# A list schedule computed at build time, DMA transposes and an earlier start for a two-layer attention and feed-forward kernel

## The chip, the cores and the metric

The kernel runs on one core of a Trainium2 chip. The metric is the device time of one execution in microseconds. Runs of one program agree within 0.3%. Short names: TensorE is PE in the profile (PEld is its weight load), VectorE is DVE, ScalarE is ACT, and SP is the engine that issues the DMAs.

## The reference

Two identical layers over x of 2,048 tokens by 1,024 columns, bf16. Each layer is local attention (32 heads of 32; a query looks at 8 keys, 2 tokens apart, backwards) and a gated feed-forward (SwiGLU) of width 3,584. Both layers use the same weights.

```
def _A_ref(x, wqkv, wo):                      # W = 8, dil = 2
    q, k, v = (x @ wqkv) split into 32 heads
    logits = einsum("bhsd,bhswd->bhsw", q, k[s - 2*w]) / sqrt(32), masked before token 0
    return softmax(logits) weighted sum of v[s - 2*w], heads joined, @ wo
def _B_ref(x, w1, w3, w2):
    return (silu(x @ w1) * (x @ w3)) @ w2
...
for _ in range(2):
    x = x + _A_ref(_layernorm(x), wqkv, wo)
    x = x + _B_ref(_layernorm(x), w1, w3, w2)
```

The pieces run in chunks of 512 tokens: Q (layer norm, q, k and v), T (attention itself, in halves of 256 tokens, on VectorE, then the projection with wo on TensorE) and B (layer norm, feed-forward). The matmuls of all chunks are 7,424 of 128x128 weights on 512 columns.

## The kernel before

A tile framework allots buffers from pools and orders the instructions of each engine; the kernel gives priorities. The parts that the change touches:

```
psQ = ...tile_pool(name="psQ", bufs=2, space=PSUM)     # PSUM banks: q/k/v and transposes
psB = ...tile_pool(name="psB", bufs=4, space=PSUM)     # feed-forward
psT = ...tile_pool(name="psT", bufs=1, space=PSUM)     # attention projection, two banks
...
def ln_chunk(c, psum):
    ...                                                # statistics, rstd
    for j in range(TPC):
        nc.vector.tensor_scalar(xn[:], x_sb[:, n, :], mv[:, j, 0:1], rstd[:, j:j + 1], ...)
        for kk in range(KT):
            nc.tensor.transpose(pT[:, kk, :], xn[:, kk * P:(kk + 1) * P], ident[:])
        nc.scalar.copy(xnT[:, :, j * P:(j + 1) * P], pT[:])
def q_stage(l, c, ln_next=None):
    for which in range(3):                             # q, k, v; weights loaded anew for each chunk
        ...
                for kk in range(KT):
                    nc.tensor.matmul(ps[:], lhsT=w[:, kk, t::KT], rhs=xnT[:, kk, :], ...)
                nc.scalar.copy(sgt[:, t - t0, :], ps[:])
            nc.sync.dma_start(qkv_d[l][which][...], sgt[:])   # to DRAM, read back by t_stage
def t_stage(l, tcx):
    nc.sync.dma_start(qT[:], qkv_d[l][0][...]); ...    # k and v likewise
    ...                                                # about 80 VectorE operations, oT
            for t in range(KT):
                nc.tensor.matmul(ps[:, hh, :], lhsT=oT[...], rhs=wo[...], ...)
def b_stage(c, last):
    for (f0, f1) in [(0, 16), (16, NF)]:               # hidden width in two parts
        ...                                            # w1, w3, Silu, product into hT, w2, x += acc
```

## Time and profile before

| | before |
|---|---|
| time, median of 3 | 1,693.61 us (1,693.15 to 1,695.7) |
| profiled span, granted clock | 1,695.0 us, 0.995 |
| N=512 matmuls x pitch | 7,424 x 215.9 ns = 1,602.5 us |
| first q matmul; first attention multiply | 13.45 us; 59.39 us |

From the page, part 1 (busy time, share of the span, instructions):

```profile
PE 1661.5 (98%) x7952; PEld 823.1 (49%) x7952; DVE 1142.3 (67%) x1930; ACT 378.7 (22%) x561; POOL 1.9 (0%) x12
```

TensorE is the bound, but 98% does not say by how much it could shrink: busy times of single matmuls overlap. The Trainium skill, too, calls the matmul busy share a poor measure of distance to the roof ("Perfetto Trace Analysis", "Identifying the Most-Contended Engine"). The chain of waits gives a better rule. Its columns are start, duration, what:

```profile
46.24 13.99 PE ps L197 x64
60.86 10.93 DMA qkv_d_2_168<-sgt
616.95 27.63 PE acc L308 x128
```

128 matmuls in 27.63 us are 215.9 ns each, the pace at which nothing is lost. So 1,602.5 us of the span are matmuls that neither kernel can avoid, and 92 us are the rest. The chain also shows the early part passing through a DMA that stores v: attention's inputs go through DRAM.

What TensorE waited for (in all, times, longest):

```profile
PE pT L132 <- DVE xn L128: 9.6, 9, 2.7
PE po L268 <- DVE oT L172: 6.5, 13, 2.2
PE ps L197 <- ACT sgt L199: 3.2, 3, 2.0
PE pT L157 <- DVE xn L154: 2.5, 3, 0.9
PE pT L132 <- DVE x_sb L313: 1.4, 1, 1.4
```

Busy time by stretch (stretch, length, then engines with counts, granted clock, DMA share, GB/s):

```profile
14.00:160.00 146.00, 137.72 (x678) 87.62 (x677) 116.31 (x205) 54.17 (x86) 0.00 (x0) 0.97 0.82 276
160.00:420.00 260.00, 256.26 (x1225) 125.94 (x1224) 254.74 (x431) 62.40 (x89) 0.00 (x0) 1.00 0.54 169
700.00:930.00 230.00, 226.85 (x1112) 114.85 (x1110) 146.36 (x248) 54.90 (x80) 0.00 (x0) 1.00 0.53 168
```

Read the counts, not the busy times. Of the 678 in the first stretch 96 are transposes (about 57 ns each), so the work is 582 x 0.2159 + 96 x 0.057 = 131 us in 146: 15 us lost. Done for all stretches after the start, the loss is 48 us. Note also that VectorE is busy for 254.7 of 260 us in the second stretch.

### The profile page before, as it was taken

What the parts mean: (1) busy time and instruction counts of PE and PEld (TensorE: products, weight loads), DVE (VectorE), ACT (ScalarE), POOL (GpSimd) and SP (SyncE); (2) the same over time, 40 slices, a digit from 0 to 9 for tenths busy, and PEclk for the clock granted to TensorE, in tenths of its full rate; (3) what the DMA queues carried; (4) which work ended last, traced back from release to release, by engine and by line L of the source; (5) the groups of instructions that cost most, each with busy time, mean ns of one, the idle gap of its engine ahead of it and who ended that gap; (6) DMA issues with size and microseconds to landing.
All of it is one profiled execution on the core that took longest, in us unless ns stands there. A gap on an engine that the chain in (4) does not pass through costs nothing.

```text
span 1695.0 us, 19762 instructions
## 1 busy us (share of the span) xinstructions
PE 1661.5 (98%) x7952; PEld 823.1 (49%) x7952; DVE 1142.3 (67%) x1930; ACT 378.7 (22%) x561; POOL 1.9 (0%) x12
## 2 busy tenths in 40 slices
PE   8999999999999999999999999999999999999999
PEld 5655644444444444554445544455444554444444
DVE  5699999999996821229982399813997159952112
ACT  3433422212213101132022321223212221121100
POOL 0000000000000000000000000000000000000000
PEclk9999999999999999999999999999999999999999
DMA  9976655554454244475434754356542654435443
GB/s 315 325 242 201 223 167 160 174 164 149 142 170 148 95 160 146 149 241 182 128 122 155 244 179 148 97 195 229 185 145 95 200 161 151 149 108 191 149 149 99
DMA packets 282891, 289.51 MB, mean 171 GB/s; under 512 B 6192, under 2 KB 256048, under 8 KB 282672
## 3 DMA queue, kind: packets, MB, share of 16 engines
q1 hardware_dynamic: 282800, 288.25, 52.7%
q8 instruction: 62, 1.02, 0.2%
q14 instruction: 29, 0.24, 0.0%
HBM read 258.87 MB, written 29.36 MB: 170 GB/s over the span
## 4 chain that ended last, share of the span: by engine, by line
PE 51%; DVE 39%; DMA 4%; issue 4%; ACT 2%; DVEq 0%; SPq 0%; ACTq 0%
PE acc L308 15%; PE pu L290 11%; PE pg L286 11%; PE ps L197 10%; DVE tm L261 6%; DVE pr L220 5%; DVE hT L295 4%; PE po L268 3%; DVE pr L170 3%; DVE tm L170 3%; DVE st L119 2%; DVE pr L171 2%; DVE tm L171 2%; DMA qkv_d_1_170<-sgt 2%; DVE x_sb L313 1%
## 5 line engine op out<-in xcount | busy, mean ns | idle before, releaser
L290 PE MATMUL pu<-xnT,w3t 128*128 128x512 bf16 x1792 | 430.9, 380 | 0.0
L286 PE MATMUL pg<-xnT,w1t 128*128 128x512 bf16 x1792 | 430.8, 380 | 0.1
L308 PE MATMUL acc<-w2t,hT 128*128 128x512 bf16 x1792 | 392.7, 379 | 0.8 <-DVE hT L295 0.8
L197 PE MATMUL ps<-xnT,wqkv 128*128 128x512 bf16 x1536 | 340.8, 382 | 4.8 <-ACT sgt L199 3.2
L294 ACT ACTIVATE sg<-pg 128x512 bf16<-128x512 f32 x224 | 133.7, 597 | 679.5 <-PE pg L286 662.9
L197 PEld LDWEIGHTS <-wqkv 128*128 128x128 bf16 x1536 | 220.2, 144 | 118.3 <-issue 10.3
L286 PEld LDWEIGHTS <-w1t 128*128 128x128 bf16 x1792 | 175.5, 98 | 209.0 <-issue 2.2
L290 PEld LDWEIGHTS <-w3t 128*128 128x128 bf16 x1792 | 175.5, 98 | 208.4 <-issue 1.6
L308 PEld LDWEIGHTS <-hT 128*128 128x128 bf16 x1792 | 174.9, 98 | 209.5 <-DVE hT L295 1.5
L220 DVE TENSOR_TENSOR pr<-qT,kT 128x2048 bf16<-128x2048 bf16 x128 | 153.6, 1213 | 170.1 <-DMA kT<-qkv_d_1_170 158.2
L295 DVE TENSOR_TENSOR hT<-sg,pu 128x512 bf16<-128x512 bf16 x224 | 152.0, 679 | 170.8 <-PE pu L290 162.7
L313 DVE TENSOR_TENSOR x_sb<-x_sb,acc 128x512 bf16<-128x512 bf16 x128 | 87.0, 681 | 147.6 <-PE acc L308 147.6
L199 ACT CAST sgt<-ps 128x512 bf16<-128x512 f32 x192 | 112.0, 586 | 229.4 <-PE ps L197 200.9
L261 DVE TENSOR_TENSOR tm<-At,vT 128x2048 bf16<-128x2048 bf16 x128 | 152.8, 1215 | 0.1
L268 PE MATMUL po<-wo,oT 128*128 128x512 bf16 x512 | 127.6, 381 | 7.8 <-DVE oT L172 6.5
L133 ACT COPY xnT<-pT 128x1024 bf16<-128x1024 bf16 x60 | 57.7, 1024 | 158.1 <-PE pT L132 153.3
L268 PEld LDWEIGHTS <-oT 128*128 128x128 bf16 x512 | 48.9, 97 | 89.8 <-DVE oT L172 39.5
L170 DVE TENSOR_TENSOR pr<-pr 128x1024 bf16<-128x1024 bf16 x128 | 86.0, 678 | 0.0
L170 DVE TENSOR_TENSOR tm<-tm 128x1024 bf16<-128x1024 bf16 x128 | 84.6, 682 | 0.0
L119 DVE BATCH_NORM_STATS2 st<-x_sb 128x6 f32<-128x512 bf16 x120 | 75.7, 672 | 6.8 <-DMA x_sb<-in_A_x_dram 6.5
L272 DVE TENSOR_TENSOR x_sb<-x_sb,po 128x1024 bf16<-128x1024 bf16 x32 | 38.7, 1210 | 25.1 <-PE po L268 25.1
L171 DVE TENSOR_TENSOR pr<-pr 128x512 bf16<-128x512 bf16 x128 | 52.2, 414 | 0.1
(203 smaller groups left out, 514.5 us busy)
## 6 DMA issues: line engine op xcount, KB each, us to landing
w1t<-in_B_w_dram SPq DMA_DIRECT2D x56, 1024.0 KB, 5.3
w3t<-in_B_w_dram SPq DMA_DIRECT2D x56, 1024.0 KB, 7.2
w2t<-in_B_w_dram SPq DMA_DIRECT2D x48, 1024.0 KB, 5.4
wqkv<-in_A_wqkv_dram SPq DMA_DIRECT2D x23, 2048.0 KB, 8.1
w2t<-in_B_w_dram SPq DMA_DIRECT2D x16, 512.0 KB, 5.1
qkv_d_0_166<-sgt SPq DMA_DIRECT2D x16, 256.0 KB, 4.8
qkv_d_1_167<-sgt SPq DMA_DIRECT2D x16, 256.0 KB, 5.0
qT<-qkv_d_0_166 SPq DMA_DIRECT2D x8, 512.0 KB, 4.8
```

The source lines that it names most:

```text
L170: nc.vector.tensor_tensor(buf[:, 0:4, :], buf[:, 0:4, :], buf[:, 4:8, :], op=ALU.add)
L171: nc.vector.tensor_tensor(buf[:, 0:2, :], buf[:, 0:2, :], buf[:, 2:4, :], op=ALU.add)
L197: nc.tensor.matmul(ps[:], lhsT=w[:, kk, t::KT], rhs=xnT[:, kk, :], start=(kk == 0), stop=(kk == KT - 1))
L199: nc.scalar.copy(sgt[:, t - t0, :], ps[:])
L220: nc.vector.tensor_tensor(pr[:], qT[:], kT[:, :, k0:k0 + TCH], op=ALU.mult)
L261: nc.vector.tensor_tensor(tm[:], At[:], win, op=ALU.mult)
L268: nc.tensor.matmul(ps[:, hh, :], lhsT=oT[:, t, j * P:(j + 1) * P], rhs=wo[:, t, hh * 512:(hh + 1) * 512], start=(t == 0), stop=(t == KT - 1))
L286: nc.tensor.matmul(pg[:], lhsT=w1t[:, kk, fi * P:(fi + 1) * P], rhs=xnT[:, kk, :], start=(kk == 0), stop=(kk == KT - 1))
L290: nc.tensor.matmul(pu[:], lhsT=w3t[:, kk, fi * P:(fi + 1) * P], rhs=xnT[:, kk, :], start=(kk == 0), stop=(kk == KT - 1))
L294: nc.scalar.activation(sg[:], pg[:], ACTF.Silu)
L295: nc.vector.tensor_tensor(hT[:, g0 + fi - f0, :], sg[:], pu[:], op=ALU.mult)
L308: nc.tensor.matmul(acc[:], lhsT=hT[:, f - f0, j * P:(j + 1) * P], rhs=w2ts[(f - f0) // 8][:, (f - f0) % 8, :], start=(f == f0), stop=(f == ...
```

## The change

The intent: write every engine's order down at build time. A small list scheduler is told a duration for each operation, plays the engines, the DMA queue and eight PSUM banks forward, and emits the operations in order of their planned start; the framework adds the semaphores only. With it come other changes. One of them is not in the cut below: the order of the stages. From the first layer's third chunk to the second layer's second, each feed-forward stage comes one chunk of q/k/v and attention later than before. The diff, cut to its core:

```
+class Program:                       # add(): reads, writes -> dependencies; place(): the plan
+    def place(self, n_banks=8, rate=330e3):
+        ...                           # earliest start first; PE picks among the heads of its lanes
+            if op.table not in (None, table):
+                t = max(t + 1.28, ready_at[op])          # ScalarE table load in the clock
+        placed.sort(key=lambda o: (o.start, o.seq))
...
-                for kk in range(KT):
-                    nc.tensor.transpose(pT[:, kk, :], xn[:, kk * P:(kk + 1) * P], ident[:])
-                nc.scalar.copy(xnT[:, :, j * P:(j + 1) * P], pT[:])
+            dma(256, xb[:, :, j * P:(j + 1) * P], xn[j][:], [("xn", j)], [("xnT", b, j)], 0, transpose=True)
...
+    def q_first():
+        load_x(0, 0, 2)
+        wslots[0] = q_weights(0, "k")
+        load_x(0, 2, 4)
+        b = ln(0, first=True)                             # this chunk still transposes on TensorE
+        order = [(0, 0, 5), (1, 0, 5), (0, 5, 8), (1, 5, 8), (2, 0, 8), (3, 0, 8)]
+        ...                                               # q of one 128-token tile at a time: 256 N=128 matmuls
+        wslots[1] = q_weights(1, "s")
+        load_x(1)
+        load_x(2, 0, 2)                                   # x ahead of wv
+        wslots[2] = q_weights(2, "s")                     # layer 0's weights stay for all four chunks
...
+                if keep:                                  # first chunk's k and v also straight to kT, vT
+                    evac(act, 0.4, lambda _, a=a, m=m: nc.scalar.copy(keep[1][:, m, HALO:], bank[a.bank][:, 0:TCH]), ...)
...
+                op = mm8(a, [(oT[oh][...], wo[...]) ...], ..., lane=1)   # projection: a lane of its own
...
-    fsplits = [(0, 16), (16, NF)] if NF > 16 else [(0, NF)]
+    hT = alloc("hT", [P, NF, CH])                         # hidden width in one part
+                pieces = pieces[:-1] + [(TPC - 1, 0, 256), (TPC - 1, 256, 128), (TPC - 1, 384, 128)]   # last tile
+    with tc.manual_schedule():
+        for op in pr.place():
+            op.emit(op)
```

## The prediction

> **What bounds it now.** TensorE. The page gives PE 98% busy, DVE 67%, ACT 22%, DMA queue 53%. There are 7,424 N=512 matmuls (groups of instructions); in the chain of waits 128 take 27.63 us, 215.9 ns each: 1,602.5 us that cannot go away. The other 92 us of the 1,695 us span: about 13.5 us before the first projection matmul (timeline), 480 later PE transposes (16 in 0.94 us in the timeline, 58 ns each, so 28 us), 3.8 us after the last matmul, and about 48 us of small losses. Counting matmuls by window (count times 216 or 58 ns against window length), the losses after the start are 15 us in 14-160 us (clock 0.97 there), 2 to 7 us in each later window, mostly at layer norms and output projections (waits: transposes on xn 9.6 us, projections on oT 6.5, ps on evacuation 3.2). VectorE sets the pace only early (254.7 of 260 us busy in 160-420); its first attention multiply waits until 59.4 us for k's round trip through DRAM.
>
> **What the change does.**
> - Layer-norm transposes after the first chunk go to DMA: 480 PE transposes (28 us of TensorE) and 60 ScalarE copies (58 us, off the path) go; 60 transfers of 256 KB are added. No trace here shows one. The Trainium skill, "DMA: Bandwidth & Descriptors", "Latency and other measured facts", states 261 GB/s for them; estimated 1 us each plus the few us to landing of ordinary ones.
> - A static list schedule on each engine, eight PSUM banks shared by all uses. Attention's projections come in blocks of 32 when all inputs should be ready: most of the 48 us goes. Its vector durations match the trace (1.22 against 1.21 us); the trace's pitch is shorter still (1.14), so real VectorE should run ahead of its plan and TensorE seldom wait for it.
> - Start: the first q is done token tile by token tile, 256 N=128 matmuls (about 15 us against 13.8), but begins when the first of four xnT tiles is there (about 9.7 us, from the first copy in the timeline), not all four (13.45), so q should end about 24.5 us against 28.9: 4 us. First k and v go straight into the attention tiles (16 extra copies of about 0.4 us, hidden): first attention multiply at about 40 us instead of 59.4. Off TensorE's path, but VectorE is then ahead of the feed-forward.
> - One feed-forward split instead of two: 64 fewer residual adds (44 us VectorE, hidden). Layer 0's qkv weights are loaded once instead of four times (18 MB less).
> - Tail: last tile cut into 256, 128, 128 columns: about 1 us.
>
> **Sum.** 24.5 us to the end of first q, plus 7,360 x 0.2159 = 1,588.8, plus 3 us tail = 1,616; plus remaining stalls, estimated 10 us (first feed-forward stage: only about 15 us of matmuls lie between the last attention projection and it, to cover adds, norm, four DMA transposes). **1,627 us**, 4% faster. Range 1,617 to 1,645. Chances: faster by over 2% 0.93, within 2% 0.06, slower by over 2% 0.01.
>
> **What would show it.** PE transposes left: 32. First q matmul at 9 to 11 us; k's first matmul at about 25 us; first pr at 38 to 42 us. DVE about 1,100 us, ACT about 325 us, DMA about 270 MB. PE's waits below 20 us in total, the largest before the first feed-forward stage.
>
> **What would make it wrong.** DMA transposes much slower than estimated, or blocking the in-order DMA queue: waits on xnT at stage starts, late weights. TensorE blocks placed too early, waiting on oT. TensorE's clock dropping in the broken-up start.

## The result

The changed kernel takes 1,617.26 us (median of 4 runs, 1,617.0 to 1,617.75) against 1,694.65 us for the one before in the same rounds. The ratio is 0.9543 (95% interval 0.9529 to 0.9556): 4.6% faster, 77.4 us between the medians. All ratios are the mean time of one kernel's fast runs over that of the other's fast runs of the same rounds, so they are not quite the ratio of the medians quoted. The outputs are correct. The time lies in the predicted range, but only 0.3 us above its lower end: 9.7 us under the point forecast.

Page, part 1:

```profile
PE 1610.0 (100%) x7716; PEld 764.4 (47%) x7716; DVE 1120.2 (69%) x1900; ACT 328.9 (20%) x519; POOL 1.9 (0%) x12
```

The chain of waits, which had 1,843 pieces before, now has 23:

```profile
23 pieces in order of time: start us, us, what
...
5.71 6.18 DMA x<-in_A_x_dram
...
24.28 1588.69 PE bank L355 x7416
1612.97 0.02 issue
1612.99 0.29 DVE x L600
```

The line of 1,588.69 us is the result in one line: from the first k matmul to the last, TensorE was never found waiting. These 7,416 matmuls hold 7,332 of N=512 and 84 narrower ones of the cut last tile. As columns they equal 7,360 of N=512, and 7,360 x 215.9 ns = 1,588.8 us. All TensorE waits (in all, times, longest) are before 16 us:

```profile
PE bank L334 <- DVE xn L320: 1.3, 2, 1.1
PE bank L278 <- DVE warm L274: 1.2, 1, 1.2
PE bank L438 <- ACT xnT L339: 0.4, 1, 0.4
```

The same stretches as before:

```profile
14.00:160.00 146.00, 145.74 (x807) 89.91 (x805) 121.72 (x219) 57.22 (x108) 0.00 (x0) 1.00 0.61 181
160.00:420.00 260.00, 260.00 (x1207) 122.71 (x1206) 229.41 (x391) 53.99 (x79) 0.00 (x0) 1.00 0.60 179
700.00:930.00 230.00, 230.00 (x1068) 104.22 (x1066) 197.08 (x337) 47.40 (x72) 0.00 (x0) 1.00 0.57 176
```

In the third stretch 1,068 matmuls fit where 1,016 and 96 transposes did before, and the clock is 1.00 throughout. The start, from the timeline (start, duration, what, and in brackets the idle time before it):

```profile
6.78 1.32 PE L334 MATMUL bank<-ident,xn 128*128 128x128 bf16 x16 [1.07 <-DVE xn L320]
8.50 6.41 PE L438 MATMUL bank<-xnT,slot 128*128 128x128 bf16 x112 [0.40 <-ACT xnT L339]
15.17 0.62 PE L334 MATMUL bank<-ident,xn 128*128 128x128 bf16 x8 [0.26 <-DVE xn L320]
24.11 36.22 PE L355 MATMUL bank<-xnT,slot 128*128 128x512 bf16 x167
```

q begins at 8.50 us and k at 24.1 us. After the last matmul 2.7 us remain to the end (3.8 before).

### The profile page after: what moved, and what is told of

Its sections match the earlier page's. It is cut to its first block, busy times and chain, and to the rows that moved or that the text cites. A ratio compares the mean times of both kernels' runs of the same rounds, so it can differ in the third digit from the quotient of the medians.

```text
span 1615.7 us, 19394 instructions
## 1 busy us (share of the span) xinstructions
PE 1610.0 (100%) x7716; PEld 764.4 (47%) x7716; DVE 1120.2 (69%) x1900; ACT 328.9 (20%) x519; POOL 1.9 (0%) x12
## 3 DMA queue, kind: packets, MB, share of 16 engines
q1 hardware_dynamic: 347728, 284.07, 57.9%
## 4 chain that ended last, share of the span: by engine, by line
PE 99%; DMA 1%; DVE 0%; SPq 0%; issue 0%
PE bank L355 98%; PE bank L438 0%; DMA x<-in_A_x_dram 0%; DMA slot<-in_A_wqkv_dram 0%; DVE st L306 0%; PE bank L334 0%; SPq L255 0%; DVE xn L320 0%; DVE mv L309 0%; DVE x L600 0%; DVE rstd L315 0%
## 5 line engine op out<-in xcount | busy, mean ns | idle before, releaser
L355 PE MATMUL bank<-xnT,slot 128*128 128x512 bf16 x5056 | 1094.2, 379 | 0.0
L355 PEld LDWEIGHTS <-slot 128*128 128x128 bf16 x5056 | 518.1, 102 | 572.9
L355 PE MATMUL bank<-slot,hT 128*128 128x512 bf16 (+2 forms) x1848 | 389.2, 373 | 0.0
L570 DVE TENSOR_TENSOR hT<-sg,bank 128x512 bf16<-128x512 bf16 x224 | 153.3, 685 | 212.5 <-PE bank L355 203.2
L259 DVE TENSOR_TENSOR scr<-scr 128x1024 bf16<-128x1024 bf16 (+3 forms) x576 | 292.2, 535 | 2.1
L568 ACT ACTIVATE sg<-bank 128x512 bf16<-128x512 f32 x224 | 133.7, 597 | 654.1 <-PE bank L355 631.0
L259 DVE TENSOR_TENSOR scr<-qT,kT 128x2048 bf16<-128x2048 bf16 x128 | 153.7, 1216 | 69.9 <-DMA kT<-qkv_d 69.9
L407 ACT CAST sgt<-bank 128x512 bf16<-128x512 f32 x184 | 107.5, 584 | 291.5 <-PE bank L355 285.3
L259 DVE TENSOR_TENSOR scr<-pA,vT 128x2048 bf16<-128x2048 bf16 x128 | 152.6, 1217 | 0.4
L355 PE MATMUL bank<-wo,oT 128*128 128x512 bf16 x512 | 113.1, 379 | 0.0
```

The costliest lines, as they stand in the source:

```text
L259: return lambda _: nc.vector.tensor_tensor(o, a, b, op=op)
L355: nc.tensor.matmul(bank[a.bank][:, 0:ncol], lhsT=w, rhs=r, start=first and i == 0, stop=last and i == n - 1)
L407: evac(act, 0.59, lambda _, a=a, i=i, m=m: nc.scalar.copy(sgt[i][:, m % 2, :], bank[a.bank][:]), op, [], [("sgt", i, m % 2)], a)
L568: evac(act, 0.6, lambda _, i=i, a=ag: nc.scalar.activation(sg[i][:], bank[a.bank][:], ACTF.Silu), og, [], [("sg", i)], ag, table="silu")
L570: evac(dve, t1(512), lambda _, i=i, a=au, f=f: nc.vector.tensor_tensor(hT[:, f, :], sg[i][:], bank[a.bank][:], op=ALU.mult), ou, [("sg", i ...
```

## The experiments

Times below are medians. The changed kernel was not rerun beside each experiment, but six variants that turned out neutral, on different occasions, lie at 1,617.2 to 1,617.8 us, so differences of 1 us and more from 1,617.26 can be read.

### Transposes back on TensorE, in the new schedule

```
-            dma(256, xb[:, :, j * P:(j + 1) * P], xn[j][:], [("xn", j)], [("xnT", b, j)], 0, transpose=True)
+            tro = pr.add("PE", 0.47, tr, [("xn", j), "ident"], [("xnT", b, j)], takes=[a], lag=0.17, lane=2)
+            evac(act, 1.0, ev, tro, [], [("xnT", b, j)], a)       # tr: 8 transposes, ev: the copy
```

> The changed kernel with the layer norms' transposes put back on TensorE (480 transposes, 60 ScalarE copies), list-scheduled. Theory A (the gain is a sum: TensorE time of the transposes, plus waits that the schedule removed, plus the start): +28 us (480 x 58 ns), so 1,645 us, TensorE still without waits, as the schedule places them as fillers. Rival B (the transposes were the source of most of the 48 us lost in the kernel before, by waits on xn, on their PSUM copies and by the dropped clock): +45 us or more. Rival C (they would have fitted for nothing): under +10 us. DMA share falls from 57.9%, which prices a DMA transpose.

1,643.9 us, ratio to before 0.9703: +26.6 us. TensorE again waits for nothing after the start. Its chain of waits shows the transposes as bare TensorE time:

```profile
54.91 1.79 PE bank L352 x32
56.70 41.44 PE bank L366 x192
98.14 1.79 PE bank L352 x32
```

32 in 1.79 us are 55.9 ns each, and 480 of them 26.8 us: theory A, within 0.2 us. The rivals fall. The DMA queue's share fell to 51.4% of 1,642.1 us, from 57.9% of 1,615.7 us: 91 us less of all 16 engines, so about 1.5 us for each of the 60 DMA transposes, or 172 GB/s (an estimate from these two shares). The Trainium skill states 261 GB/s for a transpose with a non-contiguous middle dimension, as the one here has ("DMA: Bandwidth & Descriptors", "Latency and other measured facts").

### DMA transposes alone, in the old kernel

```
-                pT = psum.tile([P, KT, P], BF16, name="pT", tag="mm")
-                for kk in range(KT):
-                    nc.tensor.transpose(pT[:, kk, :], xn[:, kk * P:(kk + 1) * P], ident[:])
-                nc.scalar.copy(xnT[:, :, j * P:(j + 1) * P], pT[:])
+                nc.sync.dma_start_transpose(xnT[:, :, j * P:(j + 1) * P], xn[:])
```

> The kernel before, with only the layer norms' transposes moved to DMA (all but the first chunk's). Theory A: -28 us of TensorE time and -12 us of the waits that name these transposes (9.6 on xn, 1.4 on x_sb, 1.1 on copies), less any new wait on xnT: 1,652 to 1,668 us. Rival B (the transposes caused nearly all losses): 1,620 to 1,640 us. Rival: DMA transposes need the new schedule to be hidden: 1,675 us or more, with TensorE waiting for xnT.

1,673.76 us against 1,693.65 us, ratio 0.988 (95% interval 0.9862 to 0.9898): a gain of 20 us, less than theory A's lower end (26 us) and more than the third theory's upper end (19 us). What TensorE waited for in this run:

```profile
PE po L265 <- DVE oT L169: 13.6, 15, 2.7
PE ps L194 <- DMA wqkv<-in_A_wqkv_dram: 7.9, 2, 6.8
PE ps L194 <- ACT sgt L196: 5.0, 5, 1.4
...
PE pg L283 <- DMA xnT<-xn: 0.8, 1, 0.8
```

The waits on xn (9.6 us) are gone, but others came in their place: on attention's output 13.6 us instead of 6.5, and on q/k/v weights 7.9 us instead of none. The weights are late because the DMA queue issues in order, and in it the transposes waited 39.9 us in all for normalised tiles (xn). The timeline of this run's DMA issues:

```profile
22.94 5.11 SPq L130 DMA_TRANSPOSE xnT<-xn  x2
...
30.30 5.63 SPq L130 DMA_TRANSPOSE xnT<-xn  x2
36.02 1.05 SPq L197 DMA_DIRECT2D qkv_d<-sgt  x2
37.16 0.45 SPq L181 DMA_DIRECT2D wqkv<-in_A_wqkv_dram  x1
```

The weight load issued here at 37.16 us was issued at 30.21 us in the kernel before. The loss by the count of the earlier section is still there: the 1,670.5 us span minus 14.0 us to the first q, 1,602.5 us of matmuls and 3.3 us of tail is 51 us, where it was 48. Part of it is new, from the DMA transposes themselves: the late weights (7.9 us), and VectorE, which now waits 23.5 us for transposes to free its two xn buffers (9.4 us before); that this is behind the longer waits on attention's output is likely, but not shown. So this run alone can't say how much of the old loss belonged to the transposes. The run before says more: with all 480 back on TensorE, but in the planned order, they bring no wait.

### Plans with other VectorE durations

One edit, three factors; only the order of instructions changes:

```
-        return pr.add("DVE", dur, emit, reads, writes, cls, **kw)
+        return pr.add("DVE", 0.75 * dur, emit, reads, writes, cls, **kw)     # or 0.9, or 1.3
```

> The changed kernel, its scheduler told that every VectorE operation takes 0.75 of what it was told before; only the order changes. In the changed kernel's trace each block of attention projections starts 0.6 to 4.3 us after its last input was ready, so the plan is nearly exact. Theory A (the removed 48 us of waits are the work of a plan with true durations): blocks now stand 56 to 450 matmuls too early, and TensorE waits for oT at most blocks; +30 to +90 us, waits of TensorE on DVE oT of that size. Rival (any static order with eight shared banks would do, VectorE has slack): under +5 us.

1,756.27 us, ratio to before 1.0362: 139 us slower than the changed kernel and slower than the one before. Theory A by direction, but beyond its range. TensorE's longest entry among the waits of this run:

```profile
PE bank L355 <- DVE oT L259: 100.2, 43, 4.6
```

The profiled execution's span is 143 us longer than the changed kernel's, so some 43 us are not waits. They fit the clock, though no run tested that alone: the mean granted clock was 0.967, and where the timeline shows a block's last 25 matmuls together after a wait they take 7.2 to 8.4 us, where 25 x 215.9 ns is 5.4:

```profile
270.03 0.61 PE L355 MATMUL bank<-wo,oT 128*128 128x512 bf16 x1 [4.21 <-DVE oT L259]
271.17 7.29 PE L355 MATMUL bank<-wo,oT 128*128 128x512 bf16 x25 [0.53 <-DVE oT L259]
```

That is what the Trainium skill leads one to expect ("TensorE: Matmul & The Clock Gate", Part 1: after an idle window of about 3.4 us the array runs at half clock, until it has been busy for about as long). The trace agrees: from 270 to 272 us the granted clock was 0.50. The expectation left it out.

> As the run with 0.75, with VectorE's durations told at 0.90. There, 16 blocks waited 6.3 us each on oT and lost about 2.4 us more each to the dropped clock. Half an attention chunk is about 55 us of VectorE, so 0.90 sets each block some 5 us early against a lead of 0.6 to 4.3 us: waits of 1 to 4 us at most blocks[...]; +20 to +55 us. Rival (the trace's VectorE pitch is 0.87 of the told durations, so 0.90 is the true plan): within 3 us.

1,617.4 us: no loss. The rival is right. With the told durations at 0.90, TensorE waits only once after the start, 0.3 us at the first block, although blocks start as little as 0.5 us after their last input. Real VectorE is faster where it matters than the plan is told, as the pitch in the trace (2.27 us for a multiply and its tree, against 2.6 us told) had said. So 0.90 (2.34 us) is nearer to the trace than the changed kernel's own plan; 0.75 (1.95 us) is 14% too short, and 1.30 (3.38 us) 49% too long.

> VectorE's durations told at 1.30. The projections of the first two attention chunks now stand directly before the feed-forward stage that needs them, with no matmuls between (in the changed kernel 72 and 136). Theory A: TensorE waits there for adds, norm and DMA transposes, 12 to 18 us each, and no wait on oT; +20 to +60 us. Rival (only an optimistic plan hurts): under +5 us.

1,742.02 us, ratio 1.0278: 125 us slower than the changed kernel, far beyond the range expected, and not without waits on oT (waits of this run):

```profile
PE bank L355 <- DMA xnT<-xn: 59.0, 7, 11.5
PE bank L355 <- DVE oT L259: 35.1, 17, 4.3
```

The 59 us are as argued: a projection too late in the order leaves nothing to do while adds, norm and transposes run. The 35 us were not foreseen: TensorE reached some blocks before oT was complete. A plan with a slow VectorE leaves TensorE idle ahead of such a block too and puts nothing else there; that is argued, not tested. The clock again stood at 0.968. So both directions hurt when they go far enough. The same instructions run in 1,617 or in 1,742 to 1,756 us, by their order (and the PSUM bank each gets with it) alone.

### One lane

```
-  ... [("oT", oh, t) for t in range(KT)] + ["wo"], lane=1)
+  ... [("oT", oh, t) for t in range(KT)] + ["wo"], lane=0)
```

> The changed kernel with attention's projections kept in the program's order on TensorE, not in a lane of their own, so that both halves of a chunk's projections stand right after the stage emitted before that chunk. Theory A: TensorE waits for whole attention chunks (about 105 us of VectorE each) where nothing was emitted between: +150 to +450 us, nearly all in waits on oT. Rival (VectorE has slack): under +50 us.

2,133.89 us (one run, state unknown): +517 us, above the range. Its main wait:

```profile
PE bank L355 <- DVE oT L259: 474.0, 47, 36.8
```

Keeping the program's order for the projections costs all overlap of attention with matmuls in several places; the mean clock fell to 0.88.

### Five banks instead of eight

```
-    def place(self, n_banks=8, rate=330e3):
+    def place(self, n_banks=5, rate=330e3):
```

> The changed kernel with five PSUM banks instead of eight for its plan. Theory A (order matters, banks only as many as a stage needs: four accumulators and one to spare): +0 to +8 us, as projection blocks are split into 16s and the w2 stages have one spare bank. Rival (the pool of eight banks removed the waits): +20 us or more, TensorE waiting on evacuations.

1,617.27 us: nothing. Sharing all eight banks is not what removed the waits.

### Table loads out of the clock

```
-  est = [(max(free[e], ready_at[o] - (1.28 if o.table not in (None, table) else 0.0)), o) for o in loose[e]]
+  est = [(max(free[e], ready_at[o]), o) for o in loose[e]]
-                t = max(t + 1.28, ready_at[op])
```

> The changed kernel with ScalarE's table loads (1.28 us, 47 of them) left out of the plan's clock. Blocks move by at most 12 places of 8 matmuls. Theory: ScalarE is 20% busy and eight banks cover a late Silu: within 1 us. Rival: a late Exp puts attention behind its plan by 1.3 us at each half, more than some leads (0.6 to 4.3 us), so TensorE waits on oT: +2 to +10 us.

1,617.2 us: nothing. This part of the change is within the plan's tolerance, as the 0.90 run also says.

### The start of the kernel before

```
-        load_x(0, 0, 2)
+        load_x(0, 0, 4)
         wslots[0] = q_weights(0, "k")
-        load_x(0, 2, 4)
-        ... (q by token tile: 256 N=128 matmuls)
+        q_tile(0, 0, 0, wslots[0], b)          # 64 N=512 matmuls when all of xnT is there
```

> The changed kernel with the start of the one before: all four x tiles first, then q's weights, and q in 64 N=512 matmuls once all four xnT tiles are there. Theory A: TensorE cannot make up lost time later, so +4 to +5 us (end of q about 28.5 to 29 us against 24.1). Rival (the start is hidden by slack later): under +1 us.

1,622.88 us: +5.6 us, a little over theory A's range. q starts at 13.99 us instead of 8.50. The timeline, then this run by stretch (columns as before):

```profile
13.99 20.18 PE L355 MATMUL bank<-xnT,slot 128*128 128x512 bf16 x85 [1.16 <-DMA slot<-in_A_wqkv_dram]
8.00:14.00 6.00, 2.52 (x25) 2.19 (x26) 3.41 (x10) 4.21 (x6) 0.00 (x0) 0.72 1.04 392
14.00:18.00 4.00, 4.00 (x11) 1.45 (x11) 0.00 (x0) 0.41 (x1) 0.00 (x0) 0.57 1.05 387
```

TensorE is mostly idle from 8 to 14 us, the granted clock drops, and q's first 4 us run at 0.57. In the changed kernel the clock stays at 1.00 there. The clock costs about 1.7 us (q takes 15.5 us, where 64 x 215.9 ns is 13.8), but it is not the excess over the range: the kernel before loses as much, its first q matmuls being 427 ns apart too, and the expected 28.5 to 29 us had that in it. The excess is a q that starts 0.5 us later than in the kernel before (13.99 against 13.45 us), because it waited for a weight slice; it ends at 29.5 us. Time lost at the start did not come back.

### k and v through DRAM

```
-            q_tile(0, 0, which, wslots[which], b, (key, tile_))
+            q_tile(0, 0, which, wslots[which], b)
...                                             # and the first half's k and v are loaded like all others
```

> The changed kernel without the direct copies of the first chunk's k and v: these go through DRAM as for other chunks. As predicted (off TensorE's path): 0 to +2 us, though the first attention multiply comes later than 47.8 us. Rival: the first feed-forward stage starts about 1 us after its last transposed tile has landed, so attention that starts 5 to 10 us later shows there as a TensorE wait of 3 to 8 us, and the time grows by as much.

1,617.54 us: +0.3 us, within the spread of the neutral variants. The direct copies are worth nothing in this kernel. Two timelines show why. The first attention multiply, changed kernel, then this run:

```profile
47.21 0.63 DVE L306 BATCH_NORM_STATS2 st<-x 128x6 f32<-128x512 bf16 x1
47.76 1.20 DVE L259 TENSOR_TENSOR scr<-qT,kT 128x2048 bf16<-128x2048 bf16 x1
```

```profile
51.03 2.36 DVE L259 TENSOR_TENSOR scr<-qT,kT 128x2048 bf16<-128x2048 bf16 x2 [2.68 <-DMA kT<-qkv_d]
```

The direct copies bring attention forward by 3.3 us only: in the changed kernel VectorE is still busy with the statistics of chunks that have just landed. And 3.3 us are no one's bottleneck: the second projection block comes 1.5 us later (168.97 against 167.44 us), and the last DMA transpose for the first feed-forward stage is issued even earlier (185.2 against 185.9 us).

### x after wv

```
-        load_x(1)
-        load_x(2, 0, 2)
         wslots[2] = q_weights(2, "s")
+        load_x(1)
+        load_x(2, 0, 2)
```

> The changed kernel with v's weights loaded ahead of the second and third chunks' x. TensorE's order is the same, instruction by instruction. Theory: chunk 1 is needed by TensorE only at 51.7 us, its last transposed tile landed at about 38 us, so 6.5 us later costs nothing: within 0.5 us. Rival: attention starts later and the first feed-forward stage, with about 1 us in hand, waits: +2 to +7 us.

1,617.55 us: nothing. The first attention multiply was no later either (47.03 us).

### An attempt at a still earlier start

```
+                    if split == "k" and (h, k) == (1, 0):
+                        load_x(0, 2, 4)                       # instead of after all eight slices
...
-                    [("x", n, hh)], [("st", q, j, hh)], pri)
+                    [("x", n, hh)] + ([("mv", q, 0)] if first and j == 1 else []), [("st", q, j, hh)], pri)
```

> An attempt at a better version: the third and fourth x tiles are loaded after four of the eight q weight slices instead of after all, and the first tile's statistics are finished before the second's begin. The chain of waits of the changed kernel runs through these x tiles (landed 11.9 us) and TensorE waits 0.26 us for them. Expected: first q matmul at 8.0 instead of 8.5 us, k's first at 23.3 to 23.6 instead of 24.1, so -0.5 to -0.8 us. If q's later weight slices come late instead, TensorE waits for slot and the gain is gone.

1,617.77 us: no gain. The timeline of this run:

```profile
6.69 0.82 PE L334 MATMUL bank<-ident,xn 128*128 128x128 bf16 x8 [0.20 <-DVE xn L320]
7.92 0.62 PE L334 MATMUL bank<-ident,xn 128*128 128x128 bf16 x8 [0.41 <-DVE xn L320]
8.61 1.95 PE L439 MATMUL bank<-xnT,slot 128*128 128x128 bf16 x32
10.79 1.96 PE L439 MATMUL bank<-xnT,slot 128*128 128x128 bf16 x32 [0.23 <-DMA slot<-in_A_wqkv_dram]
```

The first tile's transposes came 0.09 us earlier, as a statistic of the second tile slipped in ahead of its normalisation. The second tile's came 0.45 us later, and in TensorE's fixed order q stands behind both. A weight slice was also late once. k began at 24.52 instead of 24.11 us. No version faster than the changed kernel was found, and little is left: 24 us to the end of q, of which 14 are matmuls, and 2.7 us of tail.

## Why the prediction was right, point by point

- **The sum.** Predicted: 24.5 us to the end of q, 1,588.8 us of matmuls, 3 us tail, 10 us stalls. Measured: 24.1, 1,588.7 and 2.7 us, and no stalls. The error of 9.7 us is the term "plus remaining stalls, estimated 10 us". (These are times within the profiled span of 1,615.7 us; the measured time is 1.6 us longer, which the sum left out and the other terms' small errors partly offset.)
- **The mis-sized term.** It was put on the first feed-forward stage, where "only about 15 us of matmuls lie between the last attention projection and it". That reading was right: the last of the four transposes was issued at 185.9 us and the four landed in at most 5.9 us (median 4.1), and the stage began at about 190 us. But it just fits, with no wait recorded; an allowance in case of doubt became 10 us in the sum.
- **Transposes.** 28 us predicted, 26.6 us measured by putting them back: 55.9 ns each and not 58.
- **The 48 us.** Predicted to go "most"; all went. What the runs point to is the order. Shown: it is not the transposes as such (in the planned order they bring no wait), not all eight banks (five do), not the table loads; and an order planned with wrong durations brings losses of 125 to 139 us to the same kernel. So a good order is needed. That it is enough is not shown: whether the rest of the rewrite (another order of the stages, one feed-forward part, longer-lived weights, other buffers) has a share was not tested.
- **The start.** 4 us predicted (q's end at 24.5 us against 28.9). Between the two traces q's end moved from 28.9 to 24.1 us, 4.8 us; the 5.6 us of the run above hold its later start too. First q was forecast at 9 to 11 us and came at 8.5.
- **k and v direct.** Forecast "off TensorE's path": right, 0.3 us. But the first multiply was forecast for 38 to 42 us and came at 47.8: the forecast overlooked that VectorE had other chunks' statistics to do, and that q's load was issued only at 38.3 us, after DMA transposes and x loads in the queue's order.
- **"Real VectorE should run ahead of its plan."** Right in the sense that a plan with 0.90 of the durations still holds. But it does not run far ahead: the 16 projection blocks start 0.6 to 4.3 us after their last input, since VectorE's order is fixed too and it waits for TensorE's accumulators (203 us before hT alone).
- **Bytes.** 270 MB were forecast, 285 MB were moved: the forecast left out the DMA transposes' own 15.7 MB.

Of the 77.4 us, then, 26.6 are the transposes, 4.8 the start, about 1 the tail, and the remaining 45 the waits and clock drops that went with the rewrite, by all signs through the planned order (a difference, not measured by itself).

## What to carry to other kernels

When one engine bounds a kernel, count its necessary instructions times their undisturbed pitch and treat everything else as recoverable, whatever its busy share says. A static order planned with durations near those of the trace went with the recovery of nearly all of it here, but the durations of the engine that the bound one waits for must not be far off. For the multiply and its tree, plans 15% longer than the trace (the changed kernel) and 3% longer (factor 0.90) cost nothing; 14% shorter (0.75) and 49% longer (1.30) cost more than the whole gain. Not every duration mattered: the plan gave 0.45 us to the issue of a DMA transpose, which took 1.32 us (median), and TensorE still waited for none. Once the bound engine never waited, refinements elsewhere (direct copies, load order, table loads, more banks) were worth nothing.

## What the Trainium skill lacked or had wrong

- "DMA: Bandwidth & Descriptors", "Latency and other measured facts", gives 261 GB/s for DMA transposes with a non-contiguous middle dimension, from one kernel. Here 60 transposes of 128x1024 bf16 within SBUF took about 1.5 us of all engines each (172 GB/s, from two DMA shares). The page names no issue cost for one on this chip: SP was occupied for 1.26 to 3.0 us (median 1.32) per transpose, issue to landing was 3.4 us (median), and other transfers wait behind it in the queue.
- "TensorE: Matmul & The Clock Gate", "Back-to-back issue gap", gives a sustained 131 ns for an N=512 matmul with its weight load. Here it is 215.9 ns over 1,588 us without a wait, which is the page's other figure (215.7 ns). For N=128, 136 matmuls with their weight loads took 7.59 us, 55.8 ns each, not the 81 ns given there.
- "Perfetto Trace Analysis", "Identifying the Most-Contended Engine", offers two measures of distance to the roof, MFU (matmul work done as a share of the peak) and the weight loads' busy share. The second misled here: it fell from 49% to 47% while the time fell by 4.6% to a TensorE without waits. Matmul counts times pitch, which are close in kind to the first, did show the distance.
- No page that was consulted says how far a static order may be planned with wrong durations: here a factor of 0.90 on VectorE's cost nothing, 0.75 and 1.30 cost 139 and 125 us.
